# Token rows scattered one per step of the attention, and the half blocks' first layer with 128 columns of weights per product

## The chip, the cores and the metric

The kernel runs on one core of one Trainium2 chip. Its five engines work side by side and meet through semaphores: TensorE (PE in the profile; its weight loads are shown as PEld), VectorE (DVE), ScalarE (ACT), GpSimd (POOL) and SyncE (SP, which here only issues transfers). The metric is the device time of one launch in microseconds; the figure of a kernel is the median of its timed runs.

## The reference, cut to what matters

Two blocks follow one another. The first is a gated linear attention, with batch 4, 8 heads, 768 steps and head size 48:

```python
for t in range(S):
    state = alpha[:, :, t, :, None] * state + einsum('bhd,bhe->bhde', k[:, :, t], v[:, :, t])
    y[:, :, t] = einsum('bhd,bhde->bhe', q[:, :, t], state)
```

Its output, reshaped to 3072 tokens of 384 numbers, goes to a mixture of 8 experts. Each token takes the one expert whose embedding is nearest by cosine, and is scaled by that expert's probability:

```python
expert_idx = argmax(xn @ en.T / tau, axis=1)
for e in range(8):
    mask = expert_idx == e
    h = maximum(x[mask] @ w1[e], 0.0)            # 384 -> 1024
    out[mask] = gate_w[mask, None] * (h @ w2[e])  # 1024 -> 384
```

All numbers are 32-bit floats.

## The kernel before, in words

**The attention loop.** The sequence is cut into 24 chunks of 128 tokens (`NS`), and the loop at the end of the first context runs `for s in range(NS + 3)`. It is a pipeline: iteration `s` issues the loads of chunk `s + 2` (`load`), turns chunk `s` and scans its decays (`decays`, `decay_queries`), takes the scores of chunk `s - 1` (`scores`), mixes chunk `s - 2` (`mix_states`, `mix_chunk`), updates the state with chunk `s - 1` (`update`), and brings the outputs of chunk `s - 3` to token rows together with their logits (`rows`). "Step" below means the stretch from the first transpose of one chunk (`pa`) to that of the next.

POOL's part of an iteration is, in the order in which the profile shows it: the product `qs` of chunk `s` (line 513), a clearing of a buffer (line 787), the scatters of token rows if there are any (line 312), the causal mask `sm` of chunk `s - 1` (line 582), the decayed state `dec` of chunk `s - 1` (line 538), and the small product `end` (line 518). POOL runs them strictly one after another. PE needs `sm` and `dec` of a chunk one iteration later, after the scores of the next chunk.

**Routing and the scatters.** Chunks are grouped (`GROUPS`: 4, 4, 4, 2, 2, 4, 3 and 1 chunks). When the rows of a group are there, `choose` picks the expert of each of its tokens, and `place` some iterations later works out, with a few products of PE, at which row of the scratch table `xs` each token is to stand. `place` appends the group's chunks to the list `send`. A scatter (`to_rows`) is one indirect transfer issued by POOL: 128 rows of 393 numbers, each to its own row of `xs`. With `placed_at`, the groups are placed in iterations 8, 12, 16, 18, 20, 24, 25 and 26. At the end of an iteration below 23 one chunk of `send` is sent, or two when it holds more than two:

```python
n_now = len(send) if s >= NS else 0 if s == NS - 1 else 1 + (len(send) > 2)
```

So before the change iterations 8, 12, 16 and 18 send two chunks, and 9, 10, 13, 14, 17, 19, 20 and 21 send one. The context `behind(s)` places them behind the scan `a` and the product `qs` of iteration `s`. When chunk 15 has been sent, `fetch_early` lets SP fetch the first 256 tokens of the first expert. `tc.issue_after(x)` only fixes the order of instructions on `x`'s engine; it adds no semaphore.

**The experts.** After the attention, `run(i)` handles expert `i` of a list of turns: three blocks of 128 tokens each (for the first expert, one block there and two handled early). What is left of an expert's tokens, up to 64, is a half block, done by `run_extra(i)` under a condition on a register that every engine reads: `with tc.If(more > 0)`. In `half_block` the first layer computes its hidden units with the units on the partitions: 8 groups of 128 hidden units, each summed over `KT` = 3 slices of the 384 inputs. Before the change each 128 units are done as two products with 64 columns of weights, one to the upper and one to the lower 64 partitions of the result; the moving operand is the 64 tokens. Four groups share one accumulator of the pool `ps_y`, which ACT empties with a Relu (line 1238) into `hT_half`; the second layer (line 1246) follows. In the profiled input three of the eight experts, turns 0, 3 and 4, have a half block; for the other five the branch skips it.

A 32-bit product of PE shows as two records, so a half block has 96 records on line 1233 and 32 on line 1246, and as many weight loads.

Of the kernel before, what the change touches and what calls it, by code (L numbers as in the profile page):

```python
# [12 lines left out]
ALU = mybir.AluOpType  # L13
# [14 lines left out]
def kernel(  # L28
# [12 lines left out]
    nc = tc.nc  # L41
# [154 lines left out]

    def in_turn():
        return tc.issue_after(last["pe"].ins) if last else ExitStack()


    with ExitStack() as c1:
# [296 lines left out]
        def decay_queries(s):  # L498
            c = s % NCH
            d = st[s]  # L500
            L = NP * P
            pa, r = d["a"]
            rv = r.rearrange("p (n t) -> p n t", t=P)
            ini = ini_s[s % 2]
            nc.vector.reciprocal(
                ini.rearrange("p (n t) -> p n t", t=P)[:, :, 0:1], rv[:, :, 0:1]
            )
            a = work.tile([P, L], FP32, name="a")
            d["a_scan"] = by_dve = nc.vector.tensor_tensor_scan(  # L509
                a, pa, ini, 0.0, ALU.mult, ALU.add  # L510
            )
            d["qs"] = qs = work.tile([P, NP, P], FP32, name="qs", bufs=4)
            by_pool = nc.gpsimd.tensor_tensor(  # L513
                qs.rearrange("p n t -> p (n t)"), d["qc"], a, ALU.mult
            )
            if c > 0:
                d["end"] = end = work.tile([P, NP, 1], FP32, name="end", bufs=3)
                nc.gpsimd.tensor_tensor(end, rv[:, :, 0:1], al0[:, :, s : s + 1], ALU.mult)
            d["last"] = by_dve, by_pool

        def keys_back(s, ps=ps_tr, tag="tr"):
# [10 lines left out]
        def decay_state(s):  # L532

            if s % NCH == 0:
                return
            d = st[s]
            dec = d["dec"] = work.tile([P, NP, DP], FP32, name="dec", bufs=3)
            nc.gpsimd.tensor_tensor(
                dec, carried["state"], d["end"].to_broadcast([P, NP, DP]), ALU.mult
            )  # L540

# [174 lines left out]
        a0 = prepare_loads()  # L716
        prepare_fills()
        load(1)
        for s in range(NS + 3):
            if s + 2 <= NS:  # L720
                v_last = load(s + 2)
            if s + 2 == NS:

                with tc.issue_after(v_last.ins):
                    weights(0)
            if 0 <= s - 1 < NS:
                with in_turn():
                    keys_back(s - 1)
            if s < NS:
                decays(s)  # L730
            if s == NS:
                with in_turn():
                    turn_early()
            copied = None
            if s < NS:
                placing(s)
            if 3 <= s <= NS:
                with in_turn():
                    copied = rows(s - 3)
            if s < NS:  # L740
                queries(s, copied)
                decay_queries(s)
            if 0 <= s - 1 < NS:
                decay_state(s - 1)

                with in_turn(), tc.issue_after(st[s]["a_scan"].ins) if s < NS else ExitStack():
                    scores(s - 1)
            if s == 0:
                with behind(s), in_turn():
                    prepare_first(a0)  # L750
                with behind(s):
                    prepare_logits()
            if NS <= s < NS + 2:
                with in_turn():
                    first_layer_early(2 * (s - NS), 2 * (s - NS) + 1)
            if 0 <= s - 2 < NS:
                with in_turn():
                    mix_states(s - 2)
                with in_turn():
                    mix_chunk(s - 2)  # L760
            if 0 <= s - 1 < NS:

                with in_turn(), tc.issue_after(st[s]["a_scan"].ins) if s < NS else ExitStack():
                    update(s - 1)
            if 0 < s < NS and s % NCH == 0:

                with in_turn():
                    keys_back(s, ps_mm, "mm")
            if NS <= s < NS + 2:
                with in_turn():  # L770
                    first_layer_early(2 * (s - NS) + 1, 2 * (s - NS) + 2)
            if NS <= s < NS + 2:
                with in_turn():
                    rows(s - 2)
            if s == 1:
                with in_turn():
                    turn_logits()
            if s == 2:
                with behind(s):
                    routing_constants()  # L780
            if s == 3:
                with behind(s):
                    convert_constants()
            if 4 <= s < 4 + NXG * (NC + 1):
                i, t = divmod(s - 4, NC + 1)
                with behind(s):
                    nc.gpsimd.memset(xg_s[i][:, t], 0.0)
            if s == 3:
                with behind(s):
                    nc.gpsimd.memset(blank, 0.0)  # L790

            if s >= NS:
                n = placing(s)
            if lead:
                with tc.issue_after(st[s - 1]["dve"].ins):
                    next(lead[0])
                if s == S0 + 5:
                    lead.pop()
            with behind(s) if s < NS else tc.issue_after(st[NS - 1]["masked"].ins):
                n_now = len(send) if s >= NS else 0 if s == NS - 1 else 1 + (len(send) > 2)  # L800
                for c in send[:n_now]:
                    to_rows(dest[:, c : c + 1], x_g[group_of[c]][:, c - GROUPS[group_of[c]][0]])
                    send.remove(c)
                    if c == S0 - 1:
                        fetch_early()
            if s == NS:
                with tc.issue_after(st[NS - 1]["masked"].ins):
                    nc.gpsimd.memset(w1_s[1][:, 0, 0:1], 0.0)
                weights(1)
            for r in rows_of(s):  # L810
                g = group_of[r]
                if r == GROUPS[g][1] - 1:
                    with tc.issue_after(st[min(s, NS) - 1]["dve"].ins):
                        choose(g)
                    with behind(s) if s < NS else ExitStack():
                        nc.gpsimd.tensor_copy(x_g[g][:, :, TK], toks[:, slice(*GROUPS[g])])
            if s > NS:
                with in_turn():
                    first_layer_early(2 * (s - NS) + 2, 2 * (s - NS) + 4)
# [7 lines left out]
    with ExitStack() as c3:  # L827
# [42 lines left out]
            return ins  # L870

        pe = []

        def turn_of(calls):
            queue = ExitStack()
            for call in calls:
                queue.enter_context(tc.issue_after(call.ins))
            return queue

        def turn(xg, xT, n, by=None):  # L880

# [341 lines left out]
        def half_block(w1_t, w2_t, xT, gate, col):  # L1223

            hT = hp.tile([P, FT, HALF], FP32, name="hT_half", bufs=1)
            for f0 in range(0, FT, 4):
                ph = ps_y.tile([P, DM], FP32, name="pyo")[:, 0 : 4 * HALF]

                for f in range(4):
                    for k in range(KT):  # L1230
                        for i in range(2):
                            c0 = (f0 + f) * P + i * HALF
                            nc.tensor.matmul(
                                ph[i * HALF : (i + 1) * HALF, f * HALF : (f + 1) * HALF],
                                lhsT=w1_t[:, k, c0 : c0 + HALF], rhs=xT[:, k],
                                start=(k == 0), stop=(k == KT - 1), skip_group_check=True,
                            )
                nc.scalar.activation(
                    hT[:, f0 : f0 + 4].rearrange("p f t -> p (f t)"), ph, AF.Relu
                )  # L1240

            py = ps_y.tile([P, DM], FP32, name="pyo")[:, 0 : DM // 2]
            y = yp.tile([P, DM], FP32, name="y")
            for f in range(FT):
                for i in range(2):
                    nc.tensor.matmul(
                        py[i * HALF : (i + 1) * HALF], lhsT=hT[:, f],
                        rhs=w2_t[:, f, i * DM // 2 : (i + 1) * DM // 2],
                        start=(f == 0), stop=(f == FT - 1), skip_group_check=True,
                    )  # L1250
            nc.vector.tensor_scalar(y[0:HALF, 0 : DM // 2], py[0:HALF], gate, None, ALU.mult)
            nc.scalar.mul(y[0:HALF, DM // 2 :], py[HALF:], gate)
            scatter(y[0:HALF], col)
# [175 lines left out]
```

## Time and profile before

| what | value |
|---|---|
| runs, device time | 415.04, 415.48, 420.29 us; median 415.48 us |
| the profiled execution, device time | 416.3 us |
| its span, first to last instruction | 414.6 us |
| granted TensorE clock, mean | 0.988 |
| PE, share of the span | 96% |
| DVE, POOL, ACT, share of the span | 63%, 61%, 50% |
| scatters of token rows (line 312) | 24, mean 1.009 us on POOL |
| first layer of half blocks (line 1233) | 288 records, 9.9 us |
| first transposes of the first chunk, of the last one | 7.58 us, 133.23 us |

A time of the profile is counted from the start of the span. A row of a timeline gives start and length in microseconds, the engine, the line, the operation, output and inputs, the shape (rows x columns of PE's array, then the result), and how many instructions were merged; in brackets stands how long the engine had been idle, and for whom. Records of PE overlap, since products are pipelined: how fast they follow each other is read from their starts, not from their lengths.

### The profile page before, as it was taken

The numbers are of one execution on the slowest core, as the hardware profiler recorded it, in microseconds if no ns is written. First come the engines' busy times: TensorE is split into PE (matmuls) and PEld (weight loads), VectorE is DVE, ScalarE is ACT, GpSimd is POOL, SyncE is SP. The second block draws the span as 40 slices with busy tenths as digits, with TensorE's granted clock in tenths as the row PEclk, the third lists the DMA queues.
The fourth block names the chain that finished last, engine by engine and source line by source line (L and its number), as shares of the span: only waits on it lengthen the run. The fifth ranks groups of instructions, "written<-read, shape, count | busy, mean of one in ns | idle before, by whom it ended". The sixth has DMA issues, their size and how long they took to land. (4 is left out here: it accounts for less than half of the span.)

```text
span 414.6 us, 12189 instructions
## 1 busy us (share of the span) xinstructions
PE 398.9 (96%) x4688; PEld 354.6 (86%) x4688; DVE 259.3 (63%) x655; ACT 205.4 (50%) x516; POOL 252.7 (61%) x344
## 2 busy tenths in 40 slices
PE   8999999999999989999999999999999999899994
PEld 8889989888898768588979979989979979879974
DVE  4999979788889514792583572680582375374640
ACT  3455545554455532653673753662672482492520
POOL 6365687677766434771837939937837755946301
PEclk9999999999999996999999999999999999999998
DMA  9999999998986992495802903703800910100101
GB/s 140 155 166 155 155 185 188 195 193 157 191 174 125 344 371 86 136 344 180 290 16 68 344 19 115 291 19 94 315 20 21 337 50 19 40 2 16 40 16 45
DMA packets 119539, 60.26 MB, mean 145 GB/s; under 512 B 102447, under 2 KB 113976, under 8 KB 119472
## 3 DMA queue, kind: packets, MB, share of 16 engines
q1 hardware_dynamic: 115368, 49.15, 50.2%
q0 software_dynamic: 3728, 10.16, 6.9%
q8 instruction: 44, 0.72, 0.7%
q14 instruction: 23, 0.19, 0.2%
q10 hardware_dynamic: 376, 0.05, 0.1%
HBM read 49.69 MB, written 11.45 MB: 147 GB/s over the span
## 5 line engine op out<-in xcount | busy, mean ns | idle before, releaser
L990 DVE TENSOR_TENSOR hT<-hT,pq 128x384 f32<-128x384 f32 x84 | 45.5, 553 | 50.9 <-PE pq L1098 31.3
L860 POOL DMA_INDIRECT out_dram<-y,sx x25 | 24.6, 983 | 65.9 <-ACT y L995 42.4
L513 POOL TENSOR_TENSOR qs<-qc,a 128x512 f32<-128x512 f32 x24 | 30.6, 1276 | 37.0 <-DVE a L509 15.9
L1098 PE MATMUL pq<-xT_m,w_m 128*128 128x192 f32 x252 | 45.4, 326 | 0.0
L973 PE MATMUL pyo<-w,hT 128*128 128x384 f32 x128 | 42.6, 486 | 0.0
L1098 PEld LDWEIGHTS pq<-xT_m,w_m 128*128 128x128 f32 x252 | 40.8, 190 | 0.0
L973 PEld LDWEIGHTS pyo<-w,hT 128*128 128x128 f32 x128 | 24.0, 190 | 14.8
L312 POOL DMA_INDIRECT xs<-x,dest x24 | 24.2, 1009 | 17.8 <-DVE x L656 10.1
L480 DVE TENSOR_TENSOR_SCAN r<-pa,inr 128x511 f32<-128x511 f32 x24 | 29.2, 1216 | 9.0 <-PE pa L195 8.6
L995 ACT ACTIVATE hT<-hT 128x384 f32<-128x384 f32 x56 | 28.4, 518 | 12.2 <-DVE hT L990 9.6
L1010 POOL TENSOR_TENSOR w_m<-w 128x768 f32<-128x768 f32 x12 | 22.6, 1883 | 17.4 <-PE pq L1195 17.4
L1052 POOL TENSOR_TENSOR w_m<-w,w_m 128x256 f32<-128x256 f32 x42 | 30.1, 729 | 3.8 <-PE pq L1098 2.4
L192 PE MATMUL sc<-qs,kr 64*64 64x128 f32 x768 | 29.4, 273 | 2.1 <-issue 2.1
L509 DVE TENSOR_TENSOR_SCAN a<-pa,ini 128x512 f32<-128x512 f32 x24 | 29.3, 1223 | 1.1
L1195 PE MATMUL pq<-w_m,hT_m 128*128 128x192 f32 x168 | 28.5, 327 | 0.2 <-issue 0.2
L1052 POOL TENSOR_TENSOR w_m<-w 128x256 f32<-128x256 f32 x36 | 26.3, 742 | 3.7 <-PE pq L1098 2.4
L1195 PEld LDWEIGHTS pq<-w_m,hT_m 128*128 128x128 f32 x168 | 27.4, 190 | 0.5 <-issue 0.5
L192 PEld LDWEIGHTS sc<-qs,kr 64*64 64x64 f32 x768 | 22.7, 134 | 4.6 <-issue 4.2
L192 PE MATMUL pyx<-sm,vt 128*64 128x128 f32 x384 | 26.3, 279 | 0.0
L652 ACT COPY lg<-pyx 128x32 f32<-128x32 f32 x24 | 4.4, 185 | 40.8 <-PE px L192 34.7
L192 PEld LDWEIGHTS pyx<-sm,vt 128*64 128x64 f32 x384 | 20.5, 136 | 4.1 <-issue 3.6
L624 ACT COPY ycols<-pyx 128x256 f32<-128x256 f32 x48 | 17.9, 377 | 9.4 <-PE pyx L192 5.9
(230 smaller groups left out, 1003.6 us busy)
## 6 DMA issues: line engine op xcount, KB each, us to landing
w<-in_moe_w_dram SPq DMA_DIRECT2D x12, 1536.0 KB
kt<-in_k_dram SPq DMA_DIRECT2D x24, 192.0 KB
qt<-in_q_dram SPq DMA_DIRECT2D x24, 192.0 KB
vt<-in_v_dram SPq DMA_DIRECT2D x24, 192.0 KB
xg<-xs SPq DMA_DIRECT2D x22, 196.5 KB
at<-in_alpha_dram SPq DMA_DIRECT2D x24, 168.0 KB
w<-in_moe_w_dram SPq DMA_DIRECT2D x6, 512.0 KB
w<-in_moe_w_dram SPq DMA_DIRECT2D x8, 384.0 KB
```

The costliest lines, as they stand in the source:

```text
L192: last["pe"] = nc.tensor.matmul(*args, **kwargs)
L312: ins = nc.gpsimd.indirect_dma_start(out=xs, out_offset=bass.IndirectOffsetOnAxis(ap=rows, axis=0), in_=x, in_offset=None, bounds_check=E ...
L480: nc.vector.tensor_tensor_scan(r[:, L - 2 :: -1], pa[:, L - 1 : 0 : -1], inr[:, L - 2 :: -1], 1.0, ALU.mult, ALU.add,)
L509: d["a_scan"] = by_dve = nc.vector.tensor_tensor_scan(a, pa, ini, 0.0, ALU.mult, ALU.add)
L513: by_pool = nc.gpsimd.tensor_tensor(qs.rearrange("p n t -> p (n t)"), d["qc"], a, ALU.mult)
L860: ins = nc.gpsimd.indirect_dma_start(out=out, out_offset=bass.IndirectOffsetOnAxis(ap=col, axis=0), in_=y, in_offset=None, bounds_check=N - 1,
L973: pe[:] = [nc.tensor.matmul(py, lhsT=hT[:, f], rhs=w2_t[:, f], start=(f == 0), stop=(f == FT - 1),)]
L990: dve[:] = [call(*args, **kwargs)]
L995: act[:] = [call(*args, **kwargs)]
L1052: by(w[to], w[x], w[y], op)
L1098: pe[:] = [nc.tensor.matmul(to[:, f], lhsT=w[left][:, f * P : (f + 1) * P], rhs=x[right], start=start and f == 0, stop=stop, skip_group_ch ...
L1195: pe[:] = [nc.tensor.matmul(to, lhsT=left[:, f], rhs=right[:, f], start=start and f == 0, stop=stop and f == n - 1, skip_group_check=True,)]
```

## The change

There are two edits. The first sends at most one chunk at the end of an iteration. As 16 chunks no longer fit into the 14 iterations from 8 to 21 in that way, two more are sent at the beginning of iterations 18 and 20 (`TWO`), placed on POOL behind the mask of chunk `s - 2` and the last small products of chunks `s - 2` and `s - 1` (for which `d["by"]` is kept). After the change, iterations 8 to 21 send one chunk each at their end, and iterations 18 and 20 one more at their beginning. From iteration 22 on nothing changes. The second edit takes the first layer of a half block by products with 128 columns of weights. The helper `turn_of` stands earlier in the file than before.

```diff
+    def turn_of(calls):
+        queue = ExitStack()
+        for call in calls:
+            queue.enter_context(tc.issue_after(call.ins))
+        return queue
...
             if c > 0:
                 d["end"] = end = work.tile([P, NP, 1], FP32, name="end", bufs=3)
-                nc.gpsimd.tensor_tensor(end, rv[:, :, 0:1], al0[:, :, s : s + 1], ALU.mult)
+                d["by"] = nc.gpsimd.tensor_tensor(end, rv[:, :, 0:1], al0[:, :, s : s + 1], ALU.mult)
...
-            nc.gpsimd.tensor_tensor(
+            d["by"] = nc.gpsimd.tensor_tensor(
                 dec, carried["state"], d["end"].to_broadcast([P, NP, DP]), ALU.mult
             )
...
+        TWO = (S0 + 1, S0 + 3)
+
+        def send_next():
+            c = send.pop(0)
+            to_rows(dest[:, c : c + 1], x_g[group_of[c]][:, c - GROUPS[group_of[c]][0]])
+            if c == S0 - 1:
+                fetch_early()
+
         for s in range(NS + 3):
+            if s - 1 in TWO:
+                with turn_of([st[s - 2]["masked"]] + [d["by"] for d in (st[s - 2], st[s - 1]) if "by" in d]):
+                    send_next()
...
             with behind(s) if s < NS else tc.issue_after(st[NS - 1]["masked"].ins):
-                n_now = len(send) if s >= NS else 0 if s == NS - 1 else 1 + (len(send) > 2)
-                for c in send[:n_now]:
-                    to_rows(dest[:, c : c + 1], x_g[group_of[c]][:, c - GROUPS[group_of[c]][0]])
-                    send.remove(c)
-                    if c == S0 - 1:
-                        fetch_early()
+                for _ in range(len(send) if s >= NS else min(len(send), s < NS - 1)):
+                    send_next()
...
                 for f in range(4):
                     for k in range(KT):
-                        for i in range(2):
-                            c0 = (f0 + f) * P + i * HALF
-                            nc.tensor.matmul(
-                                ph[i * HALF : (i + 1) * HALF, f * HALF : (f + 1) * HALF],
-                                lhsT=w1_t[:, k, c0 : c0 + HALF], rhs=xT[:, k],
-                                start=(k == 0), stop=(k == KT - 1), skip_group_check=True,
-                            )
+                        nc.tensor.matmul(
+                            ph[:, f * HALF : (f + 1) * HALF],
+                            lhsT=w1_t[:, k, (f0 + f) * P : (f0 + f + 1) * P], rhs=xT[:, k],
+                            start=(k == 0), stop=(k == KT - 1), skip_group_check=True,
+                        )
```

More of the change, by code (lines that the diff above doesn't have):

```diff
@@ L872 @@
         pe = []
[L874 to L878, printed above, removed]
         def turn(xg, xT, n, by=None):
```

## The prediction

> **What bounds the kernel now.** I read the page first. Its rows of busy time say that PE works nearly all the span:
>
> ```profile
> PE 398.9 (96%) x4688; PEld 354.6 (86%) x4688; DVE 259.3 (63%) x655; ACT 205.4 (50%) x516; POOL 252.7 (61%) x344
> ```
>
> The chain of waits ends in PE and the last scatters and says nothing of the two places changed, so I went to the stages. For the attention I cut the span at the first transposes of chunks 5, 9, 13, 17 and 21 (busy time by stretch: the stretch, its length, then PE, PEld, DVE, ACT, POOL):
>
> ```profile
> 33.24:53.62 20.38, 20.38 (x483) 18.69 (x482) 19.04 (x36) 11.38 (x35) 12.50 (x24) 1.00 1.04 154
> 53.62:75.99 22.37, 21.77 (x499) 19.43 (x498) 18.40 (x35) 11.54 (x35) 17.06 (x29) 1.00 1.07 189
> 75.99:99.21 23.22, 22.54 (x502) 20.25 (x501) 18.39 (x35) 11.96 (x36) 16.75 (x30) 1.00 0.94 182
> 99.21:122.32 23.11, 22.24 (x489) 20.00 (x487) 19.81 (x45) 11.47 (x35) 16.41 (x25) 1.00 0.97 191
> ```
>
> The first four steps scatter nothing and take 20.38 us, with DVE busy for 19.04: DVE is the floor there. The next three stretches, which hold the scatters, are longer by 1.99, 2.84 and 2.73 us, 7.6 us together, although DVE has no more to do. The step lengths say where: chunks 9, 13, 17 and 19, each after an iteration with two scatters, take 6.88, 6.90, 5.77 and 6.59 us; chunks 10, 11, 14, 15, 18, 20, 21 and 22, with one, take 4.85 to 5.70 (mean 5.31). POOL's timeline after a pair and after a single:
>
> ```profile
> 54.52 1.18 POOL L312 DMA_INDIRECT xs<-x,dest  x1 [0.17 <-issue]
> 56.01 0.97 POOL L312 DMA_INDIRECT xs<-x,dest  x1 [0.30 <-issue]
> 56.98 0.65 POOL L582 TENSOR_SCALAR_AFFINE_SELECT sm<-sm 128x512 f32<-128x512 f32 x1
> 57.58 0.62 POOL L538 TENSOR_TENSOR dec<-state,end 128x256 f32<-128x256 f32 x1
> ...
> 60.55 1.02 POOL L312 DMA_INDIRECT xs<-x,dest  x1 [0.16 <-issue]
> 61.59 0.65 POOL L582 TENSOR_SCALAR_AFFINE_SELECT sm<-sm 128x512 f32<-128x512 f32 x1
> 62.19 0.62 POOL L538 TENSOR_TENSOR dec<-state,end 128x256 f32<-128x256 f32 x1
> ```
>
> The second scatter pushes mask and decayed state back by 1.3 to 1.5 us, to 58.2, and PE starts the product with that state (`pyx<-qs,dec`) at 57.92. PE's scores show a second loss in the same place:
>
> ```profile
> 55.55 0.73 PE L192 MATMUL sc<-qs,kr 64*64 64x128 f32 x14
> 56.59 0.46 PE L192 MATMUL sc<-qs,kr 64*64 64x128 f32 x4 [0.30 <-issue]
> 57.34 0.69 PE L192 MATMUL sc<-qs,kr 64*64 64x128 f32 x14 [0.30 <-issue]
> ```
>
> They take 2.48 us after a pair and 1.06 after the single. In every step, what ACT and PE do next starts no earlier than about 1.5 us after the start of a scatter (the copy `lg` at 57.46 after the scatter of 56.01, at 90.42 after 88.90, at 130.14 after 128.60). The trace does not say why. A single one costs PE 0.36 us (chunk 15) and 0.22 us (chunk 22), where it comes less than 0.6 us before the rows' products, and nothing where it comes earlier. So mask and scores are both late after a pair, each for about the same time; taking one away alone would free nothing.
>
> After 186 us PE has hardly a gap, and what it does longer reaches the end.
>
> **Edit 1, the scatters.** Their number stays 24, and so do their 1.01 us on POOL and about 0.5 us of all transfer engines each (software queue: 6.9% of the span over 59 transfers). Moved are four: those that were second in iterations 8, 12, 16 and 18.
>
> - Gain: a step after a pair becomes one after a single. Chunks 9 and 13: 6.9 to 5.3 us, 1.6 each. Chunk 17: 5.77 to 5.3, 0.5. Chunk 19: 6.59 to 5.5, 1.1. Sum 4.8.
> - Cost: iterations 11 and 15 get a scatter that they had not, 0 to 0.5 us each by the single ones; I take 0.3, near the 0.36 and 0.22 seen.
> - The early ones of iterations 18 and 20 stand behind mask, `dec` and `end` and ahead of `qs`. POOL is idle there for 1.96 us (to 109.26) and 2.33 us (to 121.33), against 1.2 us with the issue. If that cover is gone, `qs` is late by up to 1.2 us, but PE takes it a step later. What remains is the stall of PE, 0 to 0.5; 0.3 each.
> - Passed on the way: POOL's mask, `dec`, `end`, the memset and the copies of `choose`; of SP's queue only `fetch_early`, whose scatter stays in iteration 21, so nothing. The loads run 10 to 14 us ahead of their use. Refactoring and order edges issue nothing.
>
> Sum: -4.8 + 4 x 0.3 = **-3.6 us**. Bounds: no gain at all, if each scatter costs the same wherever it stands, and -7.6, if all the excess over the first stretch goes. What is late next is DVE, at 4.4 to 4.7 us of work per step.
>
> **Edit 2, the half blocks.** PE's timeline of the third half block, which is like the second (from 282.99 to 286.08):
>
> ```profile
> 317.57 3.25 PE L1233 MATMUL pyo<-xT,w 128*64 128x64 f32 x96
> 320.64 2.79 PE L1246 MATMUL pyo<-w,hT_half 128*64 128x192 f32 x32
> 323.36 0.59 PE L1098 MATMUL pq<-xT,w 128*128 128x192 f32 x2
> ```
>
> 96 records go in 320.64 - 317.57 = 3.07 us, two at a time (their starts lie 7 ns, then some 51 ns apart): 64 ns for a pair of records. The change leaves 48 records that run one by one. How fast? No row has 128 columns of weights and 64 moving columns at this stage. From below: 64 ns, if the 64 moving columns set the pace. From above: 213 ns, that very shape in the filler products of the first 7 us, when PE's other products were also about half as fast. Nearest by engine speed are the placing products, with 128 columns of weights and 8 to 32 moving ones (weight loads):
>
> ```profile
> 118.07 0.30 PEld L192 LDWEIGHTS pyx<-before,ones 128*128 128x128 f32 x2
> 118.29 0.30 PEld L192 LDWEIGHTS pyx<-chosen,earlier 128*128 128x128 f32 x2
> 118.51 0.30 PEld L192 LDWEIGHTS pyx<-before,ones 128*128 128x128 f32 x2
> ```
>
> Two records every 0.22 us, 111 ns each, with almost nothing to move: the weights' columns set the pace. [...]48 x 0.111 = 5.33 us, and with the 0.27 us by which today's 3.07 exceeds 48 pairs at 58 ns, 5.6 us. That is +2.5 us in turns 3 and 4. In turn 0 the second half of the layer starts at 191.06 after a wait of 0.46 us for an accumulator that DVE frees; the slower first half (2.7 in place of 1.46 us) covers it: +2.1. Sum **+7.1 us**, all on PE's path. Relu and second layer stay. SP's weight transfers that wait for this layer start later by as much, but so does PE's need for them, a whole expert later.
>
> **Edit 3, the shorter body.** The five experts without a half block jump over 256 PE instructions (96 + 96 + 32 + 32), 160 afterwards. The branches (PE's sequencer: minimum, median, maximum in ns):
>
> ```profile
> L1326 PEldq COMPARE_BRANCH  x11: 70/192/3453, 184.8 to 407.5; - x11
> ```
>
> Of the five skips three took about 0.35 us, two 2.62 and 3.45, and PE then stood 0.5 to 1.3 us longer than otherwise. [...]the two long ones could vanish, about -1.7 us. By the trace alone, where the skipped length is the same in all five and only two are long, [...]I take 0, and -1.7 to +1.5 for the range.
>
> **Sum.** Profiled execution 416.3 us (span 414.6 and 1.7 around it): 416.3 - 3.6 + 7.1 = 419.8. It lies 0.8 above the median of the runs: 415.5 + 3.5 = **419.0 us**, 0.8% slower.
>
> **The rivals.**
>
> - A, as summed: 419.0, own range 417 to 421. Chance 0.54.
> - B, the scatters give nothing: what costs is each scatter's 1.5 us hold on PE and ACT and not the pair, so spreading moves the loss into steps 12 and 16 and to the early ones. For it: single ones cost too (chunks 15, 22). Against it: of all steps up to 22 only those after a pair pass 5.9 us. 415.5 + 7.1 = 422.6. Chance 0.22.
> - C, not slower: POOL's pairs alone made the attention late, and all 7.6 us come back, since DVE sets the step again. Place: steps 9 to 20; price -7.6; it decides from a gain of 7.1 on. 415.5 - 7.6 + 7.1 = 415.0, less with shorter jumps. For it: 20.38 against 22.4 to 23.2. Against it: the rows of single scatters. Chance 0.16.
> - D, not slower: the 64 moving columns set the pace, edit 2 costs nothing, 415.5 - 3.6 = 411.9. Against it the placing products. Chance 0.05.
> - A change without effect is excluded: half blocks and pairs are in the trace. Rest, 0.03: a different order of POOL's queue that costs several us.
>
> **How the numbers follow.** The likeliest case gives 419.0. The range takes in B with +0.7 for the jumps, and C down to 415.5, leaving out D, half of C and the top of B: 415.5 to 423.3. Two per cent, about what a measurement of this kernel can tell from no change, is 8.3 us: below 407.2 lies only D with everything else in its favour, 0.01; above 423.8 the top of B and the rest, 0.06; between them 0.93.
>
> **What would show it.** Right: no step of chunks 9 to 21 above 6 us; scores of about 1.1 to 1.4 us in all of them; the last chunk's transposes near 129.6 in place of 133.2; line 1233 with 144 records that start 111 ns apart, 5.6 us per half block. Wrong: line 1233 at 58 to 64 ns per record (D); steps 12, 16, 18 and 20 longer by what 9, 13 and 19 lose (B); `qs` of chunks 18 and 20 late and PE waiting for it; other long branches.

## The result: 0.7% slower, and the profile after

On the chip on which both kernels were first compared, the changed kernel takes 418.31 us (median of 20 runs, 415.65 to 422.11) and the kernel before 415.38 us (20 runs, 413.03 to 420.29). The ratio is 1.0066, with an interval of 1.0039 to 1.0092: slower by 2.9 us. The profiled execution took 422.11 us (span 420.4 us), the slowest of the 20, so single stages of it say more than its end.

The half blocks. PE's timeline around the third one, and then the groups by shape for the new line:

```profile
321.85 5.47 PE L1239 MATMUL pyo<-xT,w 128*128 128x64 f32 x48
327.24 2.82 PE L1252 MATMUL pyo<-w,hT_half 128*64 128x192 f32 x32
```

```profile
L1239 PE MATMUL pyo<-xT,w 128*128 128x64 f32 x144 | 16.4, 274 | 0.0
L1239 PEld LDWEIGHTS pyo<-xT,w 128*128 128x128 f32 x144 | 16.5, 192 | 0.0
```

From the first record to the next layer is now 5.40 us in each half block (before: 3.50 with its wait, 3.09 and 3.07). There are 48 records, 111.7 ns apart. Mean lengths of 274 and 192 ns say nothing of this pace; the starts do.

The attention. Busy time by stretch, cut at the first transposes of chunks 5, 9, 13, 17 and 21, as before the change (columns: stretch, length, PE, PEld, DVE, ACT, POOL, granted clock, DMA share, GB/s):

```profile
33.24:53.62 20.38, 20.38 (x483) 18.68 (x481) 19.05 (x36) 11.38 (x35) 12.51 (x24) 1.00 0.99 158
53.62:75.09 21.47, 21.16 (x498) 19.21 (x497) 18.29 (x35) 11.54 (x35) 17.65 (x30) 1.00 0.79 166
75.09:99.53 24.44, 22.03 (x503) 19.65 (x502) 18.48 (x35) 11.97 (x37) 16.48 (x29) 1.00 1.01 174
99.53:121.51 21.98, 21.72 (x489) 19.63 (x488) 20.78 (x45) 11.11 (x35) 16.17 (x25) 1.00 0.99 200
```

The first and the last of the three stretches with scatters became shorter, by 0.90 and 1.13 us, and the middle one longer, by 1.22. What ends the idle time in the middle is in PE's waits from 70 to 96 us:

```profile
PE pq L195 <- DMA qt<-in_q_dram: 2.5, 4, 1.0
```

Four transposes of `q` waited for their load, 2.5 us in all, one wait in each of the chunks 12 to 15. Without them, if nothing else had been waited for, this execution would show a gain of about 3 us in the attention; with them the last chunk starts at 132.80 us, 0.4 earlier than before. SP issued the loads of `q` of chunks 13 to 15 only 6.0 to 6.1 us before PE started on them; in the kernel before it was 9.2 to 11.0 us. The last of these loads and its use:

```profile
83.25 0.65 SPq L462 DMA_DIRECT2D qt<-in_q_dram  x1
89.33 0.63 PE L195 MATMUL pq<-ident,qt 128*128 128x128 f32 x4 [0.98 <-DMA qt<-in_q_dram]
```

POOL's queue does what the edit says, one scatter, and the mask straight behind it (in these rows POOL starts each one within 0.05 us of the end of the one before):

```profile
54.55 1.19 POOL L319 DMA_INDIRECT xs<-x,dest  x1 [0.18 <-issue]
55.76 0.65 POOL L589 TENSOR_SCALAR_AFFINE_SELECT sm<-sm 128x512 f32<-128x512 f32 x1
56.37 0.62 POOL L545 TENSOR_TENSOR dec<-state,end 128x256 f32<-128x256 f32 x1
```

The branches. PE's sequencer at the conditional that skips a half block (minimum, median, maximum in ns):

```profile
L1332 PEldq COMPARE_BRANCH  x11: 70/188/358, 186.0 to 413.0; - x11
```

The two long ones (2.62 and 3.45 us) are gone, and with them 1.4 us of PE's idle time behind them.

From the first half block to the end, this pair of executions differs by 4.7 us: 6.5 us in the first layers, less 1.4 at the branches, less 0.5 at a pause of PE that comes up again below, with the profile of the kernel before on a third chip.

Between the attention and the first half block, where neither edit changes an instruction, the two executions differ as well: from the first transpose of the last chunk to the first record of the half block it is 55.89 us before the change and 57.45 after. Each lost time there in its own way. Before the change the granted clock was 0.50 for 6.8 us, and the routing's products (`phe`) followed each other half as fast (12 of them in 5.3 us; 2.7 on the third chip), some 3 us in all. After the change DVE stood for 7.0 us, and PE waited for it twice, 1.8 and 3.1 us. A busy row of the kernel before, and DVE's row of the kernel after:

```profile
155.08:161.91 6.83, 6.83 (x32) 5.66 (x24) 1.54 (x9) 1.43 (x6) 2.92 (x3) 0.50 0.30 111
173.44 0.56 DVE L895 COPY xT<-pxg 128x384 f32<-128x384 f32 x1 [6.96 <-PE pyo L981]
```

So the whole difference of this pair, 5.8 us, is -0.4 in the attention, +1.6 here and +4.7 from the first half block on. On the third chip this stretch takes 51.5 us with the kernel before and 49.7 with the changed one.

### The profile page after: what moved, and what is told of

It reads as the page before. It is cut to its first block, busy times and chain, and to the rows that moved or that the text cites. A ratio compares the mean times of both kernels' runs of the same rounds, so it can differ in the third digit from the quotient of the medians.

```text
span 420.4 us, 11901 instructions
## 1 busy us (share of the span) xinstructions
PE 399.6 (95%) x4544; PEld 356.6 (85%) x4544; DVE 261.1 (62%) x655; ACT 205.4 (49%) x516; POOL 250.6 (60%) x344
## 5 line engine op out<-in xcount | busy, mean ns | idle before, releaser
L319 POOL DMA_INDIRECT xs<-x,dest x24 | 24.4, 1016 | 13.6 <-DVE x L663 9.2
L1060 POOL TENSOR_TENSOR w_m<-w 128x256 f32<-128x256 f32 x36 | 27.6, 777 | 3.1 <-PE pq L1106 2.2
L192 PE MATMUL sc<-qs,kr 64*64 64x128 f32 x768 | 26.9, 272 | 0.0
L192 PEld LDWEIGHTS sc<-qs,kr 64*64 64x64 f32 x768 | 21.6, 133 | 0.8 <-issue 0.3
```

The lines of the kernel that those rows point to most:

```text
L192: last["pe"] = nc.tensor.matmul(*args, **kwargs)
L319: ins = nc.gpsimd.indirect_dma_start(out=xs, out_offset=bass.IndirectOffsetOnAxis(ap=rows, axis=0), in_=x, in_offset=None, bounds_check=E ...
L1060: by(w[to], w[x], w[y], op)
```

## The experiments

Every comparison below is of kernels on one and the same chip. The experiments ran on four chips, here the second to the fifth. Which chip the first comparison ran on is not known; I call it the first. The kernel before takes 415.38 us on the first and 405.54, 404.23, 404.14 and 405.29 us on the others, so ratios are comparable and times are not. That the first is a chip of its own, and not one of the four in another condition, is taken for granted here and not shown.

My theory at the outset was that of the prediction: pairs of scatters cost the attention about 4 us, and the half blocks give 7 us away. The rivals: the scatters do nothing and something else made up the difference (as B had it), or the two edits help or hinder each other.

**One edit at a time.** `e1_scatters_only` has the scatters of the change and the half blocks of before:

```diff
             with behind(s) if s < NS else tc.issue_after(st[NS - 1]["masked"].ins):
-                n_now = len(send) if s >= NS else 0 if s == NS - 1 else 1 + (len(send) > 2)
-                for c in send[:n_now]:
...
+                for _ in range(len(send) if s >= NS else min(len(send), s < NS - 1)):
+                    send_next()
```

> The scatters as after, the half blocks as before. If the prediction's first step holds, 3.6 us faster than before (ratio 0.991, 0.988 to 0.995), steps of chunks 9 to 21 all under 6 us, the last chunk's transposes at 129.6 us. If each scatter costs the same wherever it stands (rival B), no change (1.000). If all of the excess comes back (rival C), 7.6 us faster (0.982). The profile of the changed kernel, where the last chunk's transposes came only 0.4 us earlier because products waited for the loads of q in steps 12 to 15, would make it 0 to 1 us if that was no accident of one execution.

`e2_half_only` has the half blocks of the change and the scatters of before:

```diff
-                        for i in range(2):
-                            c0 = (f0 + f) * P + i * HALF
...
-                                lhsT=w1_t[:, k, c0 : c0 + HALF], rhs=xT[:, k],
...
+                            lhsT=w1_t[:, k, (f0 + f) * P : (f0 + f + 1) * P], rhs=xT[:, k],
```

> The half blocks as after, the scatters as before. If the weights' columns set the pace, 7.1 us slower than before (ratio 1.017, 1.015 to 1.019), 144 records on the half block's first layer that start 111 ns apart, 5.4 us per half block. If the moving columns did, no change. With the shorter jumps of the five experts without a half block up to 2 us less than 7.1, and the long branches of 2.6 and 3.5 us gone from the profile.

Measured on the second chip: the scatters alone 405.31 us, ratio 1.0004 (0.9983 to 1.0026); the half blocks alone 411.53 us, ratio 1.0171 (1.0122 to 1.0219), which is 6.9 us (4.9 to 8.9 by the interval; the medians differ by 6.0). The half blocks cost what was forecast (7.1), as far as six runs tell. The scatters are worth nothing there.

`e5_after_again` is the changed kernel and `e6_before_again` the kernel before, each without an edit, on a third chip.

> The changed kernel once more, unaltered. The two edits alone gave 1.000 (scatters) and 1.017 (half blocks) against before where before took 405.5 us; both together gave 1.0066 where before took 415.4 us. If the edits add and what the scatters are worth depends on the chip, this gives about 1.017 where before takes about 405 us and its profile has no step in which the scores after a scatter take longer than 1.1 us; and 1.005 to 1.009 where before takes about 415 us. If instead the two edits together do something that neither does alone, it is 1.007 on either chip.

> The kernel before, unaltered, for its profile on this chip. Where it takes about 405 us: scores of 1.06 us after every pair of scatters, steps of chunks 9, 13, 17 and 19 at 4.9 to 5.7 us, the last chunk's transposes at 128 to 130 us. Where it takes about 415 us: scores of 2 to 2.6 us after the pairs again, and steps of 5.8 to 6.9 us.

Both edits together: 411.14 us, ratio 1.0166 (1.012 to 1.0212), 6.9 us (difference of the medians). So, within these intervals, the edits add up, and neither hides the other. The kernel before took 403.98 us in the run that was profiled (span 402.3 us), and its attention is another one than on the first chip. The same stretches, the first of which agrees with the first chip to 0.01 us:

```profile
33.24:53.62 20.38, 20.38 (x483) 18.69 (x482) 19.04 (x36) 11.38 (x35) 12.49 (x24) 1.00 0.96 149
53.62:74.72 21.10, 21.05 (x498) 19.07 (x497) 18.27 (x35) 11.54 (x35) 17.00 (x29) 1.00 1.08 189
74.72:96.10 21.38, 21.38 (x503) 19.67 (x502) 18.30 (x35) 11.95 (x36) 16.75 (x30) 1.00 0.95 188
96.10:117.00 20.90, 20.90 (x488) 19.37 (x487) 19.70 (x45) 11.47 (x35) 16.38 (x25) 1.00 1.04 208
```

The stretches with scatters are 22.37, 23.22 and 23.11 us long on the first chip and 21.10, 21.38 and 20.90 here, with the same instructions and almost the same busy time of DVE, ACT and POOL (within 0.13 us). What is different shows behind the first pair. POOL's timeline on the third chip:

```profile
54.52 1.18 POOL L312 DMA_INDIRECT xs<-x,dest  x1 [0.17 <-issue]
56.01 0.97 POOL L312 DMA_INDIRECT xs<-x,dest  x1 [0.31 <-issue]
56.99 0.64 POOL L582 TENSOR_SCALAR_AFFINE_SELECT sm<-sm 128x512 f32<-128x512 f32 x1
57.60 0.62 POOL L538 TENSOR_TENSOR dec<-state,end 128x256 f32<-128x256 f32 x1
```

and PE's in the same microseconds:

```profile
55.55 1.06 PE L192 MATMUL sc<-qs,kr 64*64 64x128 f32 x32
56.44 0.62 PE L192 MATMUL pyx<-qs,dec 64*64 64x128 f32 x16
56.98 1.26 PE L192 MATMUL pyx<-sm,vt 128*64 128x128 f32 x14
```

POOL's four rows are those of the first chip to within 0.02 us: the mask starts at 56.99 and the decayed state at 57.60. But PE takes its scores in 1.06 us, not 2.48, and the products behind them in time. These use the decayed state and the mask of the chunk before, which are long done: `pyx<-qs,dec` starts at 56.44, the `dec` of this step only at 57.60. The delay on POOL is the same on both chips and costs PE 0.27 us at most on this one (chunk 9, in the table below). The step of chunk 9 is 5.62 us long here and 6.88 on the first chip. So what made the pairs dear was the second thing that the prediction saw: PE pauses in the middle of its scores, and ACT's next copies come only about 1.5 us after the second scatter's start (`lg` at 57.46 on the first chip, at 55.78 on the third). I call it the hold. The first chip shows it in both kernels. In all other profiles the scores of chunks 4 to 22 take at most 1.11 us, with one exception of 1.26 (`e9_scatters_again`).

Step lengths in us, from the starts of the transposes (chunks that follow a pair before the change are 9, 13, 17 and 19; the extra scatters of the change bear on 12, 16, 18 and 20):

| kernel, chip | 9 | 12 | 13 | 16 | 17 | 18 | 19 | 20 | 8 to 22 together |
|---|---|---|---|---|---|---|---|---|---|
| before, first | 6.88 | 5.28 | 6.90 | 5.72 | 5.77 | 5.27 | 6.59 | 5.48 | 84.89 |
| after, first | 5.48 | 5.78 | 6.58 | 5.71 | 4.85 | 5.60 | 5.83 | 5.70 | 84.46 |
| before (e6), third | 5.62 | 5.28 | 5.39 | 5.72 | 4.85 | 5.27 | 5.32 | 5.48 | 79.37 |
| after (e5), third | 5.35 | 5.28 | 5.32 | 5.71 | 4.85 | 5.27 | 5.63 | 6.01 | 80.62 |
| scatters alone (e1), second | 5.35 | 5.28 | 5.32 | 5.71 | 4.85 | 5.27 | 5.63 | 5.51 | 79.44 |

Without the hold a pair costs 0.27 us in chunk 9, 0.07 in chunk 13 and nothing in 17 and 19; there is no more to be won by taking the pairs apart, and the early scatter makes chunk 19 longer by 0.31.

The profile of `e6_before_again` also tells where 6.9 us come from. Its third half block:

```profile
306.54 3.02 PE L1233 MATMUL pyo<-xT,w 128*64 128x64 f32 x96
309.39 2.77 PE L1246 MATMUL pyo<-w,hT_half 128*64 128x192 f32 x32
```

2.85 us there, 2.92 in turn 0 (3.0 to 5.0 in the other profiles with old half blocks, by a wait for DVE in its middle) and 5.40 in the changed kernel: 2.48 + 2.55 + 2.55 = 7.6 us. One thing goes back. In the second layer of a full turn between the first and the second half block, PE paused before the change:

```profile
235.60 4.14 PE L1195 MATMUL pq<-w_m,hT_m 128*128 128x192 f32 x24 [0.42 <-issue]
```

The distance between the two starts is 0.75 us there, 0.52 on the first chip. Every profile with the old half blocks has this pause, of 0.5 to 1.4 us, and none of the four with the new ones (`after`, `e2`, `e5`, `e10`) has it. From the end of the first half block to the start of the second, 87.4 us become 86.6. The sum is 7.6 - 0.75 = 6.9 us.

**Other places for the scatters.** If pairs cost nothing, it should not matter which pairs are parted. `e3_first_pairs` parts only those of iterations 8 and 12:

```diff
-                n_now = len(send) if s >= NS else 0 if s == NS - 1 else 1 + (len(send) > 2)
+                n_now = len(send) if s >= NS else 0 if s == NS - 1 else 1 + (len(send) > 2 and s >= S0)
```

> Before, but iterations below 16 send one scatter each at most; the pairs of iterations 16 and 18 stay and nothing is sent early. By the prediction's step: chunks 9 and 13 gain 1.6 us each, iterations 11 and 15 cost 0.3 each, 2.6 us faster (0.994). If a scatter costs the same wherever it stands, no change. If this gains as much as or more than the scatters of the change as a whole, the two early ones and the undone pairs of 16 and 18 are worth nothing.

`e4_behind_mask` takes the scatters to the start of the next iteration, behind the mask and not ahead of it, but for two more at the ends of iterations 17 and 19:

```diff
+            if 0 < s < NS and send:
+                with turn_of([st[s - 2]["masked"]] + [d["by"] for d in (st[s - 2], st[s - 1]) if "by" in d]):
+                    send_next()
...
+                for _ in range(len(send) if s >= NS else min(len(send), s in TWO)):
+                    send_next()
```

> Half blocks as before; one scatter per iteration from 9 on, queued on POOL behind the mask of the chunk before instead of ahead of it (two more at the ends of iterations 17 and 19). If a pair is dear because it keeps mask and decayed state back in POOL's queue, this is at least as good as one scatter ahead of the mask: 4 to 7 us faster than before (0.983 to 0.990). If it is dear because PE and ACT stand until 1.5 us after the start of a scatter, the scatters now start about 1 us later, over the rows' products and scores, and each step loses 0.4 to 1 us: same as before or slower (1.000 to 1.015).

Measured, on the second chip: 405.48 us, ratio 0.9999 (0.9978 to 1.002), and 405.77 us, ratio 1.0000 (0.9977 to 1.0022). Neither gives anything. In the second, POOL's queue put the scatter between mask and decayed state. In both the profile shows longer steps at chunks 18 and 20 (6.35 and 6.81, 6.25 and 6.07 us). For the first kernel, PE's waits from 70 to 125 us say why:

```profile
PE pq L195 <- DMA qt<-in_q_dram: 2.1, 2, 1.2
```

Single transposes that wait 0.3 to 1.2 us for a load of `q` turn up in some step between 12 and 22 of most kernels here, with the old scatters too (`e2_half_only` at 91.9 and 124.9 us). `e1_scatters_only` has none, `e9_scatters_again` one with the same program. But of the four profiles in which the pairs stand one shows such waits, and of the eight in which pairs are taken apart six do. That spreading the scatters makes loads late, and so eats up what it wins, is a rival that no run here excludes.

**The price of a scatter by itself.** `e7_each_twice` is the kernel before with each of the 16 scatters of iterations 8 to 21 issued twice:

```diff
+    xs2 = nc.dram_tensor("xs2", (E * N + NROW, ROW), FP32, kind="Internal").ap()
...
+                    if c < S0:
+                        to_rows(dest[:, c : c + 1], x_g[group_of[c]][:, c - GROUPS[group_of[c]][0]], xs2)
```

> Before, with each of the 16 scatters of the attention issued a second time straight behind the first, into a spare table that nobody reads, so 16 scatters more. Theory (a scatter by itself costs PE little where no hold is seen; POOL has the room): 0 to 0.3 us each, 0 to 5 us in all, ratio 1.00 to 1.012; with the hold 0.4 to 1.5 us each, 6 to 24 us in all, ratio 1.015 to 1.06. Rival (a pair costs what it delays in POOL's queue: mask and decayed state 1.3 us later each time): steps with two now longer by 1.3 us and those with four by 2.6 us, over 16 us in all, without any score longer than 1.1 us.

Measured, on the fourth chip: 415.47 us against 404.14, ratio 1.0273 (1.022 to 1.0326), 11.3 us. Neither side had this right. Against the step lengths of `e6_before_again`, steps 8 to 22 are longer by 10.3 us, and this is not spread evenly: chunks 9 and 10 together by 2.6, 13 and 14 by 2.5, 17 and 18 by 2.1, 19 and 20 by 2.9, all the others together by 0.2. Two scatters in an iteration by themselves (10, 14, 20, 21) are free; four, followed by two in the next iteration, are not. Busy time of two such steps and of the next one:

```profile
53.62:59.26 5.64, 5.57 (x131) 4.88 (x130) 4.09 (x7) 3.03 (x9) 4.68 (x7) 1.00 1.35 205
59.26:67.19 7.93, 6.10 (x131) 5.15 (x129) 4.62 (x8) 3.13 (x9) 7.44 (x11) 1.00 1.09 253
67.19:72.12 4.93, 4.93 (x126) 4.38 (x124) 4.80 (x12) 3.00 (x9) 4.37 (x10) 1.00 1.27 212
```

and POOL's timeline in the long one, from the row that ends the backlog of four scatters on:

```profile
60.83 1.28 POOL L515 TENSOR_TENSOR qs<-qc,a 128x512 f32<-128x512 f32 x1
62.04 0.43 POOL L789 MEMSET xg<- 128x393 f32 x1
62.64 1.02 POOL L314 DMA_INDIRECT xs<-x,dest  x1 [0.16 <-issue]
63.96 0.97 POOL L314 DMA_INDIRECT xs<-x,dest  x1 [0.31 <-issue]
64.94 0.65 POOL L584 TENSOR_SCALAR_AFFINE_SELECT sm<-sm 128x512 f32<-128x512 f32 x1
```

POOL is busy for 7.44 of 7.93 us and has become the bound. `qs` of chunk 9 comes 7.2 us after the start of its step instead of 4.7 (`e6_before_again`), the mask behind two more scatters starts only at 64.94, and from 53 to 90 us PE waits for masks:

```profile
PE pyx L194 <- POOL sm L584: 3.2, 2, 1.8
```

The scores of chunks 5 to 22 take 1.06 to 1.11 us in this profile, so there is no hold in it (those of chunk 23 take 2.03, with no scatter near them). So here POOL's queue did cost PE time, as the prediction thought, with its slack used up. In the kernel before POOL has about 1 us of slack per step (17.00 us busy in the four steps of 21.10), and a pair is followed by steps that let it catch up.

**Which columns set the pace.** `e10_half_the_columns` is the changed kernel with 32 of the 64 token columns moved in the first layer; ACT copies their results into the places of the other 32:

```diff
-                            ph[:, f * HALF : (f + 1) * HALF],
-                            lhsT=w1_t[:, k, (f0 + f) * P : (f0 + f + 1) * P], rhs=xT[:, k],
+                            ph[:, f * HALF : f * HALF + HALF // 2],
+                            lhsT=w1_t[:, k, (f0 + f) * P : (f0 + f + 1) * P], rhs=xT[:, k, 0 : HALF // 2],
```

> After, with the half blocks' first layer moving 32 of its 64 token columns; the other 32 take the same values by a second copy, so half of these tokens get wrong rows. Theory (the 128 columns of weights set the pace): 48 records still 111 ns apart, 5.4 us per half block. Rival (the moving columns set it): about 2.7 us per half block, and the run some 8 us faster than after.

Measured, in one run on the fourth chip: 419.42 us, slower by 15.3 us than the kernel before, which neither side foresaw: the changed kernel loses 6.9. In the second half block the first 39 records start 111.7 ns apart (from the second on), as with 64 columns. That is the theory's answer: the columns of weights set the pace. Then something else sets in. The half block cut in three, at 4.2 us, and where the second layer begins (columns as above):

```profile
277.69:281.85 4.16, 4.16 (x40) 4.16 (x39) 0.00 (x0) 0.80 (x3) 3.82 (x4) 1.00 0.13 47
281.85:284.02 2.17, 2.17 (x13) 2.10 (x12) 0.00 (x0) 0.00 (x0) 0.83 (x1) 0.52 0.27 95
284.02:288.83 4.81, 4.81 (x32) 3.62 (x32) 0.00 (x0) 0.45 (x2) 0.00 (x0) 0.51 0.66 228
```

The granted clock goes to half although PE is busy all the time, the records follow each other by 213 ns, and the second layer, which is unaltered, takes 4.81 us in place of 2.8, at a granted clock of 0.51 (0.65 and 0.66 in the other two half blocks). It happens in all three half blocks, 5.9, 4.3 and 5.1 us after their start (they are 10.6, 11.4 and 9.7 us long, against 8.2 with 64 columns); the last two can be seen in the page's row of slices:

```profile
PEclk9999999999999999999999999996999899999998
```

With 64 columns the clock is 1.00 in all three half blocks of `after` and in the second one of `e5_after_again`; over the whole span of `e2_half_only` its mean is 1.000.

**The scatters alone, on two more chips.** `e9_scatters_again` and `e11_scatters_third` are `e1_scatters_only` without a further edit. I wanted the gain of the scatters measured by itself where the hold is seen.

> The scatters of after with the half blocks of before, as in the first of these experiments. Theory (what a pair costs depends on whether PE and ACT stand still around a scatter, which some chips show and others not): where the profile shows the scores of paired steps at 2.5 us, a ratio near 0.990; where it shows 1.06 us everywhere, 1.000. Rival (the first chip's smaller loss had another cause, such as long branches of PE): 1.000 whatever the scores show.

> The scatters of after with the half blocks of before once more, for whether the gain of some 4 us that the scatters seem to have had where the two kernels were first compared is seen with a kernel that changes nothing else. Theory (PE and ACT standing around a scatter is what a pair costs, and only some chips show it): where scores behind a scatter take 1.3 us and more in the profile, 0.990; where all take 1.06 us, 1.000 to 1.0025 as in the two runs before. Rival (the scatters are worth nothing anywhere): 1.000 to 1.0025 also where such long scores are seen.

Measured: 405.62 us, ratio 1.0025 (1.0003 to 1.0047), on the fourth chip, and 405.26 us, ratio 1.0002 (0.9977 to 1.0027), on a fifth. All scores take 1.06 us, with one exception of 1.26: no hold here either. Both results are what the theory says for chips without it; its other half, 0.990 on a chip that shows the hold, stays untried.

## Why the prediction was right, and where its reasons were not

The time, 419.0 us, came out at 418.3, and the likeliest case, A, gives about the sum that the first chip shows. Its terms fared differently: one is right with its reason, the other came near on one chip with half of its reason wrong. That the sum came so close is in part luck.

- **Half blocks, +7.1 us: right, mechanism and size.** 48 records at 111.7 ns, and it costs 6.9 us on two chips (intervals from 4.9 to 8.9). Inside the sum three things were off by less than a microsecond. The 0.27 us that I carried over as an edge does not recur (5.40 us per half block, not 5.6). The pairs of 64 columns take 2.85 us when nothing disturbs them, less than the 3.07 that I read. And a pause of 0.5 to 0.75 us in a later turn goes away, which I had not seen in the profile. The row of the placing products was the right measure (111 ns there, 111.7 here). That the moving columns set the pace is refuted by the equal pace, 111.7 ns, at 64 and 32 of them, and rival D falls with it.
- **Scatters, -3.6 us: near it on the first chip only, and for half of the reason.** The step that failed is "mask and scores are both late after a pair, each for about the same time; taking one away alone would free nothing". The mask is just as late on the third chip, where PE takes its scores in 1.06 us: it is needed a step later, and the lateness fits into POOL's slack. The product at 57.92, which the prediction gave as waiting for the state of 57.58, takes the state of the chunk before. The hold made the steps long. It is also narrower than "in every step" says: on the same chip PE starts 49 records within 1.5 us of the scatter at 54.52, and ACT a copy 0.15 us after the one at 60.55. Where there is no hold, the term is 0 to +1.0 us, which is rival B's outcome for a reason that B didn't have.
- **How much it is on the first chip is not settled.** If the half blocks cost 6.9 us there too, the rest of the change gave back about 4.2 (2.7 by the ratio, less 6.9). Part of this may be the branches: the two profiled executions differ by 1.4 us at them. So the scatters gave some 2.8 to 4.2 us there. This is argued from a difference and was not measured by itself; the intervals alone leave about 1 to 7 us. The pair of profiles can't settle it: it shows 0.4 us in the attention, and between the attention and the half blocks each execution lost several us to something else.
- **The gain per step and the cost of the added scatters.** On the first chip, chunks 9, 13, 17 and 19 lost 1.40, 0.32, 0.92 and 0.76 us, 3.4 together, where 4.8 was forecast; chunk 13 still took 6.58 us (0.67 of it for a late load), and chunk 15, with another late load, 6.50. So two of the signs named for "right" did not come: no step above 6 us, and the last chunk near 129.6 (it came at 132.80). Of the 4 x 0.3 us for the added ones, chunks 16, 18 and 20 show 0.0, 0.33 and 0.22; chunk 12's 0.50 has a late load of 0.3 in it.
- **The loads, put at nothing.** The prediction let them run 10 to 14 us ahead of their use and named DVE as what is late next. The loads of `q` ran 9 to 11 us ahead before the change and 6 after it, and in chunks 12 to 15 PE waited 2.5 us for them. On the third chip they run 5.9 to 7.4 us ahead in chunks 13 to 15 of both kernels and nothing waits, so a short lead alone doesn't make them late.
- **Jumps, 0 with -1.7 to +1.5: near its lower end in the pair of profiles, 0 in the other comparison of both edits.** Most skips cost the same 0.47 us from start to start, with either length of body. Long branches are in two of the eight profiles with the old half blocks, the first one of the kernel before and `e4_behind_mask`, where PE's records stand 1.10 us apart at it (the row below), and in none of the four with the new ones. Since the skipped body is as long in the other six, its length alone doesn't make a branch long. That a shorter body could make the long ones vanish was my estimate, priced at the 1.7 us for which PE waited behind the two; no trace shows that it does, and whether it keeps them away stays open.

```profile
L1334 PEldq COMPARE_BRANCH  x11: 70/193/2896, 176.3 to 398.3; - x11
```

Rival C, that all 7.6 us come back, fails on the first chip: late loads and what is left of the hold (scores of up to 1.45 us) keep the stretches at 21.5 to 24.4 us. On the third chip, the kernel before already sits at 20.9 to 21.4 us.

Nothing tried beats the kernel before by a measurable amount. The scatters of the change with the half blocks of before should be the better choice where the hold is seen, which was not tried; on the three chips where it ran it is no faster.

## What to carry to other kernels

Here, where weights change with every product and few columns move, the pace is that of the columns of weights: two products of 64 columns on two halves of the array, side by side, beat one of 128 by nearly two to one (59 ns for the pair against 112). So count weight columns, not instructions, before merging small products. A late result on a side engine was no loss here as long as its consumer's start did not move with it: on the third chip mask and decayed state come as late after a pair as on the first (56.99 and 57.60 us), and a pair costs 0 to 0.27 us. So look up when the consumer reads the result, and how much slack the engine's queue has per step (about 1 us for POOL here). And before a stall is priced as a property of the kernel, have the unaltered kernel profiled on a second chip: here nearly all of the stall, 5.5 us in steps 8 to 22, was seen on the first alone.

## What was unexpected of the hardware

- **PE and ACT stood still around scatters on one chip.** On the first chip, PE pauses in its scores and ACT's copies start about 1.5 us after a scatter (scores of 1.42 to 2.64 us after pairs and one single in the kernel before); in the profiles of the four other chips the same 32 records take at most 1.11 us in chunks 4 to 22, with one exception of 1.26. The kernel before is 10 to 11 us slower there. In the two profiles of it 5.5 us of that lie in steps 8 to 22, and 4.4 between the attention and the first half block: some 3 by the granted clock of 0.50, and 1.7 in a wait of PE for a copy of ACT, behind four scatters in a row. Why it happened is open; it was seen in one set of executions, and no run here could bring it about.
- **The granted clock was lost while PE was busy.** With 128 columns of weights and 32 moving columns, back to back for 4.3 us in the second half block, the clock fell to 0.52, and PE's records show no gap ahead of it (PE busy for 4.16 of 4.16 us); with 64 moving columns it stayed at 1.00 for 5.4 us. Where the clock fell to 0.50 in the kernel before on the first chip, PE had been busy for 8.12 of the 10.08 us ahead of it, and the longest pause was 1.73 us. Whether it goes by the amount moved is open; two sizes don't show it.
